# Hash attention and a gated feed-forward block: one pool of two-bank PSUM tiles for both phases, with sums and hashes sharing a tile

## The chip, the cores and the metric

The kernel runs on one core of one Trainium2 chip. The metric is the device time of one launch in microseconds (us). Five engines work side by side: TensorE (PE in the profile; its weight loads are PEld), VectorE (DVE), ScalarE (ACT), GpSimd (POOL) and SyncE (SP, which here only issues transfers). PSUM is the memory into which TensorE writes its results; it has eight banks of 512 fp32 values in each of 128 partitions. An instruction waits on semaphores for the instructions of other engines on which it depends.

## The reference

```python
# attention: B, H, S, D = 4, 8, 768, 64; proj is (64, 6)
q_bits = (np.einsum('bhsd,dk->bhsk', q, proj) > 0)          # the same for k
q_bucket = np.sum(q_bits * 2 ** np.arange(6), axis=-1)
mask = q_bucket[:, :, :, None] == k_bucket[:, :, None, :]
scores = np.where(mask, (1 / np.sqrt(D)) * np.matmul(q, k.transpose(0, 1, 3, 2)), -1e9)
attn = np.exp(scores - np.max(scores, axis=-1, keepdims=True))
attn = attn / (np.sum(attn, axis=-1, keepdims=True) + 1e-9)
x = np.matmul(attn, v).transpose(0, 2, 1, 3).reshape(3072, 512)
# feed-forward block: w_gate and w_val (512, 1536), w_out (1536, 512)
g = x @ w_gate
out = (g * (1 / (1 + np.exp(-g))) * (x @ w_val)) @ w_out
```

## The kernel before

The kernel has two phases, traced one after the other. The order in which each engine gets its instructions is the order of the program text (a manual schedule); every wait between engines is put in from the tiles that an instruction reads and writes. A pool hands out its tiles in turn from a fixed number of slots, and the first write into a slot waits for all users of the tile that had it before.

**Attention** goes over 16 pairs of heads (n = 0 to 15). A pair has 12 units: two halves of 384 query columns, and in each six chunks of 128 keys. Its PSUM pool has eight one-bank tiles (`bank`). An iteration n of the loop issues, in this order:

- for each of the 12 units `score`: `products` takes two bank tiles, one for each head, and writes q times k into them in fp32; `mark` adds a bf16 product of the hash bits, which shifts the pairs of unlike buckets out of reach, and then issues the exponential, one ACTIVATE of 384 columns for each head (L524), into a ring of 12 weight tiles A. Between the units, `add` sums these weights on VectorE;
- `total(n-1)`: matmuls with a column of ones reduce the sums of the pair before (`sum`, L578), ScalarE copies them to SBUF (`row`, L581), and transfers and a reciprocal on VectorE (`invert`) prepare the division (`norm`) for the next iteration;
- `prepare_pair(1)`, while there is a next pair: the hash matmuls of pair n+1 (`hps`, L423) into one bank tile, the signs on ScalarE (L428), a spread of the q bits by a transfer on POOL's queue (L440) and of the k bits on VectorE (L437);
- a step of the preparation of the feed-forward weights (`begin_pieces`, `advance_pieces`), which are split into three parts and kept in DRAM;
- for each of the 12 units `attend`: the weights times v (`av`, L539). Each half of a pair has a bank tile of its own, and ScalarE copies it to `xT` (L549) when its six chunks are done; `mean` (L548) is a small copy beside it.

The first pair is treated apart (`start_first`): it has transposes on TensorE (`tps`), and nine idle matmuls run ahead of them.

**The gated block** goes over three blocks of 1024 tokens. Each block has 12 steps U: the gate and the value product, each with a tile `a` (16 matmuls, the main parts) and a tile `n` (8 matmuls, the parts to be subtracted), then the evacuation, Silu and product, which leave `hid` in three parts h, l and d (L737, L740, L742). After each three steps there is a product D with `w_out`: eight chunks of 128 tokens, where `first` (six matmuls with h and l, into bank 0 of a tile `o`) and `second` (three with d, into bank 1) are evacuated by L785 and L789 on VectorE. In the last D of a block the first four chunks are begun ahead of time with two of the three `hid` tiles (`ahead` = 4), while the third is still being made. In the last D of all, chunks from the fifth on run `second` ahead of `first`, and the eighth (`last`) is worked in two halves of 256 columns, each with its own store (L816). This phase's PSUM pool has four two-bank tiles (`two_banks`), opened when the first phase's pool is closed.

Of the kernel before, what the change touches and what calls it, by code (L numbers as in the profile page):

```python
# [8 lines left out]
FP32 = mybir.dt.float32  # L9
# [10 lines left out]
def kernel(  # L20
# [54 lines left out]
    RINGS = (3, 3)  # L75
    ringp = [ctx.enter_context(tc.tile_pool(name="ringp", bufs=RINGS[0]))]
    dram = ctx.enter_context(tc.tile_pool(name="dram", bufs=1, space=bass.MemoryType.DRAM))
    ctx.enter_context(tc.manual_schedule())

    halves = [slice(half * HQ, (half + 1) * HQ) for half in range(2)]  # L80

# [216 lines left out]
    def attention(scope):  # L298
# [2 lines left out]
        fixed = scope.enter_context(tc.tile_pool(name="fixed", bufs=1))  # L301
        att = scope.enter_context(tc.tile_pool(name="att", bufs=2))
        xp = scope.enter_context(tc.tile_pool(name="xp", bufs=4))
        banks = scope.enter_context(tc.tile_pool(name="ps", bufs=8, space=PSUM))

        def bank(name):
            return banks.tile([P, 512], FP32, tag="ps", name=name)

        pairs = [(b, pr) for b in range(B) for pr in range(NP)]
        raws = {}  # L310
# [52 lines left out]
        nc.vector.memset(zeros, 0.0)  # L363
        for t in (sides["k", 0], sides["q", 0], sides["q", 1]):
            nc.vector.memset(t, 0.0)
        for _ in range(9):
            ps = bank("idle")
            nc.tensor.matmul(ps, zeros[:, 0:P], zeros[:, 0:512], start=True, stop=True)

        HR = 16  # L370
        assert 2 * NBITS <= HR and 2 * HR == BLOCK
# [40 lines left out]
        T = {}  # L412
        bits = {}

        def front(n):
            bits["q", n] = sides["q", n % 2]
            bits["k", n] = sides["k", n % 2]
            low, high = slice(0, BLOCK), slice(D, D + BLOCK)

            def hash_blocks(todo):  # L420
                tile_ = bank("hps")
                for i, (name, half) in enumerate(todo):
                    nc.tensor.matmul(tile_[i * BLOCK : (i + 1) * BLOCK, 0:HQ], hash_w,  # L423
                                     T[name, n][:, half * HQ : (half + 1) * HQ],
                                     start=True, stop=True)

                def sign(i, name, half, to=low, **how):
                    nc.scalar.activation(bits[name, n][to, half * HQ : (half + 1) * HQ],  # L428
                                         tile_[i * BLOCK : (i + 1) * BLOCK, 0:HQ], AF.Sign,
                                         **(how or {"bias": nudge[name]}))  # L430

                return [lambda i=i, at=at, **how: sign(i, *at, **how) for i, at in enumerate(todo)]
# [20 lines left out]
            def start_first():  # L453
                for half in range(2):
                    cols = slice(half * HQ, (half + 1) * HQ)
                    for name in "kq":
                        if not half:
                            T[name, n] = opnd.tile([P, S], FP32, tag=name + "T", name=name + "T")
                        ps = bank("tps")
                        for i in range(CH):  # L460
                            nc.tensor.transpose(ps[:, i * P : (i + 1) * P],
                                                raws[name, n][:, half * CH + i].rearrange("p h d -> p (h d)"),
                                                ident)
                        if name == "k":
                            nc.scalar.activation(T[name, n][:, cols], ps[:, 0:HQ], AF.Copy,
                                                 scale=2 / OFF)
                        else:
                            nc.vector.tensor_copy(T[name, n][:, cols], ps[:, 0:HQ])

                def both_heads(sign, name, half):  # L470
                    cols = slice(half * HQ, (half + 1) * HQ)
                    sign()
                    if name == "k":
                        spread_k(mask, cols)
                    else:
                        nc.vector.tensor_copy(bits["q", n][high, cols], bits["q", n][low, cols])

                products(0)
                todo = [("k", 0), ("q", 0), ("k", 1), ("q", 1)]
                signs = hash_blocks(todo)  # L480
                for i in range(3):
                    both_heads(signs[i], *todo[i])
                products(1)
                products(2)
                mark(0)
                both_heads(signs[3], *todo[3])
                mark(1)
                mark(2)

# [13 lines left out]
        def weights(u):  # L503
            return ring[u % RING]
# [3 lines left out]
        def product(u, x, start):  # L508
            n, half, c = units[u]
            qs = slice(half * HQ, (half + 1) * HQ)  # L510
            ks = slice(c * P, (c + 1) * P)
            for h in range(2):
                rows = slice(h * D, (h + 1) * D)
                nc.tensor.matmul(banks_of[u][h], x["k", n][rows, ks], x["q", n][rows, qs],  # L514
                                 start=start, stop=not start)

        def products(u):
            banks_of[u] = [bank("sc")[:, 0:HQ] for _ in range(2)]
            product(u, T, True)

        def mark(u):
            product(u, bits, False)
            for h, sc in enumerate(banks_of.pop(u)):
                nc.scalar.activation(weights(u)[:, h, 0:HQ], sc, AF.Exp,  # L524
                                     scale=SCALE * (1.0 if units[u][0] else OFF / 2))

        def score(u):
            products(u)
# [2 lines left out]
        def attend(u):  # L531
            n, half, c = units[u]
            a = weights(u)
            if c == 0:
                av[n] = bank("av")
            ps = av[n]
            width = AW if half == 0 else HQ
            for h in range(2):
                nc.tensor.matmul(ps[h * D : (h + 1) * D, 0:width], raws["v", n][:, h, c, :],  # L539
                                 a[:, h, 0:width], start=c == 0, stop=c == NCH - 1)  # L540
            if c == NCH - 1:
                if half == 0:
                    if n == len(pairs) - 1:
                        xT[n] = lastp.tile([P, S], FP32, tag="last", name="lastx")
                    else:
                        xT[n] = xp.tile([P, S], FP32, tag="xT", name="xT")
                    mean[n] = small.tile([P, 1], FP32, tag="e", name="e")
                    nc.scalar.activation(mean[n], ps[:, HQ : HQ + 1], AF.Copy, scale=EPS)  # L548
                nc.scalar.copy(xT[n][:, half * HQ : (half + 1) * HQ], ps[:, 0:HQ])  # L549

        both = {}

# [17 lines left out]
        sums = [dram.tile([P, each], FP32, tag=f"sums{i}", name="sums") for i in range(2)]  # L570

        def total(n):
            ps = bank("sum")
            t = [acc.pop((n, half)) for half in range(2)]
            for h in range(2):
                for half in range(2):
# [93 lines left out]
    def gated_block(scope):  # L670
# [2 lines left out]
        hidp = scope.enter_context(tc.tile_pool(name="hidp", bufs=4))  # L673
        outp = scope.enter_context(tc.tile_pool(name="outp", bufs=1))
        homes.append(outp)
        pp = scope.enter_context(tc.tile_pool(name="pp", bufs=4, space=PSUM))

        def two_banks(name):
            return pp.tile([P, 2, 512], FP32, tag="pp", name=name)

        hids = {}
        accs = {}
        rows = [out[b * S : (b + 1) * S, :].rearrange("(p c) m -> p c m", c=NCH) for b in range(B)]
# [2 lines left out]
        def mm(ps, w, x, start, stop):  # L686
            nc.tensor.matmul(ps, w, x, start=start, stop=stop)  # L687
# [27 lines left out]
        def atoms_of(kind, n):  # L715
# [33 lines left out]
            else:  # L749
# [2 lines left out]
                hs = [hids[NQ * n + j] for j in range(NQ)]  # L752
                tiles = {}

                def start(c, js):
                    if c not in tiles:
                        tiles[c] = two_banks("o")
                    t = tiles[c]
# [8 lines left out]
                        for j in js:  # L767
                            mm(t[:, 1], hs[j][:, 2, cols], ws[j][:, 2], j == 0, j == NQ - 1)

                    for go in (second, first) if final and c >= ahead else (first, second):  # L770
                        go()

                def end(c):
                    t = tiles.pop(c)
# [23 lines left out]
                for c in range(ahead):  # L798
                    yield lambda c=c: start(c, range(NQ - 1))
                def last(c):  # L800
                    t, tn = two_banks("o"), two_banks("o")
                    cols = slice(c * P, (c + 1) * P)
                    for j in range(NQ):
                        mm(tn[:, 0], hs[j][:, 2, cols], ws[j][:, 2], j == 0, j == NQ - 1)
                    nc.vector.tensor_tensor(accs[c], accs[c], tn[:, 0], op=ALU.subtract)
                    batch, at = divmod(b * NCB + c, NCH)
                    for half in range(2):
                        here = slice(half * DM // 2, (half + 1) * DM // 2)
                        for j in range(NQ):
                            for v in range(2):  # L810
                                mm(t[:, half, 0 : DM // 2], hs[j][:, v, cols], ws[j][:, v, here],
                                   j == 0 and v == 0, j == NQ - 1 and v == 1)
                        nc.vector.scalar_tensor_tensor(out=accs[c][:, here], in0=t[:, half, 0 : DM // 2],  # L813
                                                       scalar=STEP + 1, in1=accs[c][:, here],
                                                       op0=ALU.mult, op1=ALU.add)
                        nc.sync.dma_start(rows[batch][:, at, here], accs[c][:, here])  # L816

                for c in range(NCB):
# [2 lines left out]
                        return  # L821

                    def chunk(c=c):
                        start(c, [NQ - 1] if c < ahead else range(NQ))
                        end(c)
                    yield chunk

# [95 lines left out]
```

## Time and profile before

| | |
|---|---|
| median of 3 runs | 913.97 us (913.93 to 914.4) |
| profiled execution | 914.08 us |
| its span in the profile | 912.0 us, at a granted TensorE clock of 0.999 |
| TensorE busy | 904.2 us (99%) |
| VectorE busy | 667.2 us (73%) |
| ScalarE busy | 453.8 us (50%) |
| GpSimd busy | 97.0 us (11%) |
| attention phase | to 317.34 us, where the first matmul of the gated block starts |

The span runs from the first to the last record of the core; the execution's time has 2.1 us beside it. A row of the profile page names the line, engine, operation and tiles, then the busy time, the mean length of one, and the idle time of the engine ahead of it with what ended that. A row of the timeline has the start, the duration and what ran. The end of a matmul is modelled, and neighbours overlap: a matmul with 512 columns shows as 389 ns and follows the one before at 227 ns.

### The profile page before, as it was taken

To read this page: it belongs to the slowest core of one execution; us is meant where nothing else is said; L and a number is where in the kernel's file an instruction comes from. 1 tells how busy PE (TensorE), PEld (TensorE's weight loads), DVE (VectorE), ACT (ScalarE), POOL (GpSimd) and SP (SyncE) were. 2 spreads that over 40 slices of the span, in tenths; PEclk is the share of its full clock that TensorE was granted. 3 is DMA by queue.
4 is the path that set the end of the run, shared out by engine and by line. 5 is a ranking of instruction groups with operands and counts; after the bars stand their busy time and mean duration, and the time that the engine had idled before them with its cause. 6 is when DMAs were issued, how large, how long until landed. Compare 5 with 4: busy or idle time off the path is not lost.

```text
span 912.0 us, 12995 instructions
## 1 busy us (share of the span) xinstructions
PE 904.2 (99%) x4795; PEld 638.8 (70%) x4795; DVE 667.2 (73%) x774; ACT 453.8 (50%) x812; POOL 97.0 (11%) x193
## 2 busy tenths in 40 slices
PE   9999999999999999999999999999999999999997
PEld 5444444444444488888888788888888888888886
DVE  5999999998989768679776756464658754574746
ACT  6889888788887655452414133322313233313230
POOL 1011101010111210001000000101010100010000
PEclk9999999999999999999999999999999999999999
DMA  8677797778886699686756563434444642525232
GB/s 185 127 199 204 212 210 174 173 209 233 216 192 208 209 374 334 224 283 208 279 198 235 206 232 104 181 132 173 138 148 152 239 157 99 185 73 210 99 138 93
DMA packets 145582, 174.28 MB, mean 191 GB/s; under 512 B 106496, under 2 KB 115200, under 8 KB 145520
## 3 DMA queue, kind: packets, MB, share of 16 engines
q0 software_dynamic: 22864, 116.36, 36.4%
q1 hardware_dynamic: 121056, 56.71, 24.8%
q8 instruction: 38, 0.62, 0.3%
q10 hardware_dynamic: 1600, 0.39, 0.2%
q14 instruction: 24, 0.20, 0.1%
HBM read 133.17 MB, written 39.42 MB: 189 GB/s over the span
## 4 chain that ended last, share of the span: by engine, by line
PE 97%; DVE 2%; DMA 0%; ACTq 0%; ACT 0%; issue 0%; DVEq 0%
PE a L687 29%; PE o L687 20%; PE sc L514 17%; PE n L687 14%; PE av L539 14%; PE sum L578 1%; PE hps L423 1%; DMA kraw<-in_k_dram 0%; DVE hid L742 0%; DVE hid L740 0%; DVE v L732 0%; DVE v L736 0%; DVE xparts L292 0%; ACTq L329 0%; ACT hid L737 0%
## 5 line engine op out<-in xcount | busy, mean ns | idle before, releaser
L687 PE MATMUL a<-xparts,ring 128*128 128x512 f32 x1152 | 273.0, 389 | 0.6 <-ACT row L581 0.6
L687 PEld LDWEIGHTS a<-xparts,ring 128*128 128x128 f32 x1152 | 216.2, 188 | 46.2 <-ACT row L581 1.3
L687 PE MATMUL o<-ring,hid 128*128 128x512 f32 (+1 forms) x870 | 199.0, 388 | 2.3 <-DVE o L813 1.2
L687 PEld LDWEIGHTS o<-ring,hid 128*128 128x128 f32 x870 | 162.5, 188 | 37.2 <-DVE hid L742 2.4
L524 ACT ACTIVATE A<-sc 128x384 f32<-128x384 f32 x384 | 155.9, 504 | 8.1 <-PE sc L514 7.3
L514 PE MATMUL sc<-qT,kT 64*128 64x384 f32 x768 | 157.5, 488 | 0.0
L687 PE MATMUL n<-xparts,ring 128*128 128x512 f32 x576 | 142.3, 389 | 0.0
L539 PE MATMUL av<-A,vraw 128*64 128x386 f32 (+1 forms) x768 | 127.7, 488 | 0.0
L687 PEld LDWEIGHTS n<-xparts,ring 128*128 128x128 f32 x576 | 108.1, 188 | 22.4
L732 DVE TENSOR_TENSOR v<-v,n 128x1024 f32<-128x1024 f32 x36 | 44.0, 1221 | 99.4 <-PE n L687 98.8
L244 POOL DMA_DIRECT2D ring<-ram x108 | 56.9, 529 | 501.2 <-PE n L687 329.2
L539 PEld LDWEIGHTS av<-A,vraw 128*64 128x64 f32 x768 | 53.7, 137 | 73.3 <-issue 61.4
L514 PEld LDWEIGHTS sc<-qT,kT 64*128 64x128 f32 x768 | 70.3, 187 | 47.8 <-issue 41.9
L726 ACT ACTIVATE g<-a 128x1024 f32<-128x1024 f32 x36 | 36.9, 1026 | 132.1 <-PE a L687 127.2
L737 ACT ACTIVATE hid<-v 128x1024 fp32r<-128x1024 f32 x36 | 38.2, 1062 | 114.8 <-DVE v L736 114.8
L734 ACT ACTIVATE g<-g 128x1024 f32<-128x1024 f32 x36 | 38.2, 1061 | 85.2 <-DVE g L732 85.2
L789 DVE TENSOR_TENSOR o<-o 128x512 f32<-128x512 f32 x92 | 63.0, 687 | 20.6 <-ACT o L783 18.2
L732 DVE TENSOR_TENSOR g<-g,n 128x1024 f32<-128x1024 f32 x36 | 43.8, 1216 | 33.3 <-PE n L687 33.3
L514 PE MATMUL sc<-qb,kb 64*128 64x384 bf16 x384 | 66.0, 323 | 0.0
L560 DVE SCALAR_TENSOR_TENSOR both<-A 128x1536 f32<-128x1536 f32 x32 | 55.8, 1744 | 7.4 <-ACT A L524 6.1
L564 DVE TENSOR_TENSOR both<-both,A 128x1536 f32<-128x1536 f32 x32 | 56.2, 1757 | 3.2
L740 DVE SCALAR_TENSOR_TENSOR hid<-hid,v 128x1024 fp32r<-128x1024 f32 x36 | 44.0, 1223 | 19.2 <-ACT hid L737 19.1
(79 smaller groups left out, 701.0 us busy)
## 6 DMA issues: line engine op xcount, KB each, us to landing
ring<-ram POOLq DMA_DIRECT2D x108, 768.0 KB, 4.8
ram<-stage POOLq DMA_DIRECT2D x23, 768.0 KB, 5.6
ram<-stage SPq DMA_DIRECT2D x13, 768.0 KB
qraw<-in_q_dram SPq DMA_DIRECT2D x64, 96.0 KB
vraw<-in_v_dram SPq DMA_DIRECT2D x16, 384.0 KB
out_dram<-o SPq DMA_DIRECT2D x23, 256.0 KB
kraw<-in_k_dram SPq DMA_DIRECT2D x60, 96.0 KB
r<-sums SPq DMA_DIRECT2D x30, 192.0 KB
```

The costliest lines, as they stand in the source:

```text
L244: nc.gpsimd.dma_start(t.bitcast(FP32), ram[at].bitcast(FP32))
L514: nc.tensor.matmul(banks_of[u][h], x["k", n][rows, ks], x["q", n][rows, qs], start=start, stop=not start)
L524: nc.scalar.activation(weights(u)[:, h, 0:HQ], sc, AF.Exp, scale=SCALE * (1.0 if units[u][0] else OFF / 2))
L539: nc.tensor.matmul(ps[h * D : (h + 1) * D, 0:width], raws["v", n][:, h, c, :], a[:, h, 0:width], start=c == 0, stop=c == NCH - 1)
L560: nc.vector.scalar_tensor_tensor(out=t, in0=first, scalar=S * EPS / P / 2, in1=now, op0=ALU.add, op1=ALU.add)
L564: nc.vector.tensor_tensor(t, t, now, op=ALU.add)
L687: nc.tensor.matmul(ps, w, x, start=start, stop=stop)
L732: nc.vector.tensor_tensor(two(z), two(z), n_, op=ALU.subtract)
L734: nc.scalar.activation(z, z, AF.Silu)
L737: nc.scalar.activation(h, val, AF.Copy, scale=TOWARD / STEP)
L740: nc.vector.scalar_tensor_tensor(out=l, in0=h.bitcast(FP32), scalar=-STEP, in1=val, op0=ALU.mult, op1=ALU.add)
L789: nc.vector.tensor_tensor(accs[c], accs[c], t[:, 1], op=ALU.subtract)
```

## The change

The four two-bank tiles become the only PSUM pool, opened once for both phases.

- A unit of scores takes one such tile, a bank for each head, and one ACTIVATE of 768 columns makes the exponential of both.
- Both halves of `av` lie in one tile. `mean` and the copy to `xT`, now one of 768 columns, are issued after the last chunk of the second half.
- `joint(n)` is a tile that is made on first use. `total(n)` writes the sums of pair n into its bank 0, and the hash matmuls of pair n+2 go into its bank 1. In iteration n these are the sums of pair n-1 and the hashes of pair n+1, so both use `joint(n-1)`. The order of the calls in the loop is as before.
- The nine idle matmuls alternate between the banks of one tile, and each `tps` uses one bank of a tile.
- In the last D of each block, `first` of chunks 0 and 1 is completed ahead of `second` of chunk 0.
- `last` takes three tiles: one for the parts to be subtracted and one for each half.

```diff
+    pp = ctx.enter_context(tc.tile_pool(name="pp", bufs=4, space=PSUM))
     ctx.enter_context(tc.manual_schedule())
+
+    def two_banks(name):
+        return pp.tile([P, 2, 512], FP32, tag="pp", name=name)
...
-        banks = scope.enter_context(tc.tile_pool(name="ps", bufs=8, space=PSUM))
-
-        def bank(name):
-            return banks.tile([P, 512], FP32, tag="ps", name=name)
...
-        for _ in range(9):
-            ps = bank("idle")
-            nc.tensor.matmul(ps, zeros[:, 0:P], zeros[:, 0:512], start=True, stop=True)
+        idle = two_banks("idle")
+        for i in range(9):
+            nc.tensor.matmul(idle[:, i % 2], zeros[:, 0:P], zeros[:, 0:512], start=True, stop=True)
...
+        joints = {}
+
+        def joint(n):
+
+            if n not in joints:
+                joints[n] = two_banks("joint")
+            return joints[n]
+
         def front(n):
...
             def hash_blocks(todo):
-                tile_ = bank("hps")
+                tile_ = joint(n - 2)[:, 1]
...
-                        ps = bank("tps")
+                        ps = two_banks("tps")[:, 0]
...
-                nc.tensor.matmul(banks_of[u][h], x["k", n][rows, ks], x["q", n][rows, qs],
+                nc.tensor.matmul(banks_of[u][:, h], x["k", n][rows, ks], x["q", n][rows, qs],
                                  start=start, stop=not start)
 
         def products(u):
-            banks_of[u] = [bank("sc")[:, 0:HQ] for _ in range(2)]
+            banks_of[u] = two_banks("sc")[:, :, 0:HQ]
             product(u, T, True)
 
         def mark(u):
             product(u, bits, False)
-            for h, sc in enumerate(banks_of.pop(u)):
-                nc.scalar.activation(weights(u)[:, h, 0:HQ], sc, AF.Exp,
-                                     scale=SCALE * (1.0 if units[u][0] else OFF / 2))
+            nc.scalar.activation(weights(u)[:, :, 0:HQ], banks_of.pop(u), AF.Exp,
+                                 scale=SCALE * (1.0 if units[u][0] else OFF / 2))
...
-            if c == 0:
-                av[n] = bank("av")
-            ps = av[n]
+            if (half, c) == (0, 0):
+                av[n] = two_banks("av")
+            ps = av[n][:, half]
...
-            if c == NCH - 1:
-                if half == 0:
...
-                    mean[n] = small.tile([P, 1], FP32, tag="e", name="e")
-                    nc.scalar.activation(mean[n], ps[:, HQ : HQ + 1], AF.Copy, scale=EPS)
-                nc.scalar.copy(xT[n][:, half * HQ : (half + 1) * HQ], ps[:, 0:HQ])
+            if (half, c) == (1, NCH - 1):
...
+                mean[n] = small.tile([P, 1], FP32, tag="e", name="e")
+                nc.scalar.activation(mean[n], av[n][:, 0, HQ : HQ + 1], AF.Copy, scale=EPS)
+                nc.scalar.copy(xT[n].rearrange("p (x q) -> p x q", x=2), av[n][:, :, 0:HQ])
...
         def total(n):
-            ps = bank("sum")
+            ps = joint(n)[:, 0]
...
-        pp = scope.enter_context(tc.tile_pool(name="pp", bufs=4, space=PSUM))
-
-        def two_banks(name):
-            return pp.tile([P, 2, 512], FP32, tag="pp", name=name)
...
-                def start(c, js):
+                def start(c, js, steps=None):
...
-                    for go in (second, first) if final and c >= ahead else (first, second):
-                        go()
+                    for go in steps or ("ba" if final and c >= ahead else "ab"):
+                        (first if go == "a" else second)()
...
                 def last(c):
-                    t, tn = two_banks("o"), two_banks("o")
+                    tn, *ts = (two_banks("o")[:, 0] for _ in range(3))
...
-                        mm(tn[:, 0], hs[j][:, 2, cols], ws[j][:, 2], j == 0, j == NQ - 1)
-                    nc.vector.tensor_tensor(accs[c], accs[c], tn[:, 0], op=ALU.subtract)
+                        mm(tn, hs[j][:, 2, cols], ws[j][:, 2], j == 0, j == NQ - 1)
+                    nc.vector.tensor_tensor(accs[c], accs[c], tn, op=ALU.subtract)
...
-                                mm(t[:, half, 0 : DM // 2], hs[j][:, v, cols], ws[j][:, v, here],
+                                mm(ts[half][:, 0 : DM // 2], hs[j][:, v, cols], ws[j][:, v, here],
                                    j == 0 and v == 0, j == NQ - 1 and v == 1)
-                        nc.vector.scalar_tensor_tensor(out=accs[c][:, here], in0=t[:, half, 0 : DM // 2],
+                        nc.vector.scalar_tensor_tensor(out=accs[c][:, here], in0=ts[half][:, 0 : DM // 2],
...
                     def chunk(c=c):
-                        start(c, [NQ - 1] if c < ahead else range(NQ))
+                        if c >= ahead:
+                            start(c, range(NQ))
+                        elif c == 0:
+                            start(0, [NQ - 1], "a")
+                            start(1, [NQ - 1], "a")
+                            start(0, [NQ - 1], "b")
+                        else:
+                            start(c, [NQ - 1], "b" if c == 1 else "ab")
                         end(c)
```

More of the change, by code (lines that the diff above doesn't have):

```diff
@@ L540, in attend @@
                                  a[:, h, 0:width], start=c == 0, stop=c == NCH - 1)
-            if c == NCH - 1:
-                if half == 0:
[L543 to L546, printed above, removed]
-                    mean[n] = small.tile([P, 1], FP32, tag="e", name="e")
-                    nc.scalar.activation(mean[n], ps[:, HQ : HQ + 1], AF.Copy, scale=EPS)
-                nc.scalar.copy(xT[n][:, half * HQ : (half + 1) * HQ], ps[:, 0:HQ])
+            if (half, c) == (1, NCH - 1):
+                pool, tag = (xp, "xT") if n < len(pairs) - 1 else (lastp, "last")
+                xT[n] = pool.tile([P, S], FP32, tag=tag, name=tag)
+                mean[n] = small.tile([P, 1], FP32, tag="e", name="e")
+                nc.scalar.activation(mean[n], av[n][:, 0, HQ : HQ + 1], AF.Copy, scale=EPS)
+                nc.scalar.copy(xT[n].rearrange("p (x q) -> p x q", x=2), av[n][:, :, 0:HQ])
         both = {}
```

## The prediction

> **What bounds the kernel now.** I read the busy times first, then the waits of TensorE, then the timeline of one pair in the attention phase, of the handover between the phases, and of the end. From the profile page:
>
> ```profile
> PE 904.2 (99%) x4795; PEld 638.8 (70%) x4795; DVE 667.2 (73%) x774; ACT 453.8 (50%) x812; POOL 97.0 (11%) x193
> ...
> L524 ACT ACTIVATE A<-sc 128x384 f32<-128x384 f32 x384 | 155.9, 504 | 8.1 <-PE sc L514 7.3
> ```
>
> PE (TensorE) is busy for 904.2 of 912.0 us. Whatever relieves ACT (ScalarE), which is half idle, brings nothing by itself; a change counts only where it opens or closes a gap of PE. The waits of PE (engine, line waited for: us in total, times, longest) are these, apart from 0.3 us at the first transpose:
>
> ```profile
> PE idle L368 <- DVE kb L363: 1.3, 1, 1.3
> PE o L687 <- DVE o L813: 1.2, 1, 1.2
> PE o L687 <- DVE hid L742: 1.1, 3, 0.4
> PE a L687 <- ACT row L581: 0.6, 1, 0.6
> ```
>
> So the most that can be won is small: the last chunk (L813), the last product of each of three blocks (L742), the handover (L581). In the attention phase PE has no wait at all. The timeline of pair 7 (start, duration) shows how its engines hand over:
>
> ```profile
> 153.06 0.33 PE L514 MATMUL sc<-qb,kb 64*128 64x384 bf16 x2
> ...
> 153.32 0.85 PE L578 MATMUL sum<-acc,ones 128*32 128x384 f32 x8
> ...
> 153.99 0.49 PE L423 MATMUL hps<-qT,hash 128*32 128x384 f32 x2
> ...
> 154.31 0.48 ACT L581 COPY row<-sum 128x384 f32<-128x384 f32 x1
> ...
> 154.75 0.54 PE L539 MATMUL av<-A,vraw 128*64 128x386 f32 x2
> ```
>
> The reader is to see that the hash matmuls (hps) start at 153.99, 0.32 us **before** the copy that reads the sums (row) starts. The two lie in different tiles. Pairs 1 to 14 all show this order, with the row copy 0.95 to 0.99 us after the first sum matmul.
>
> Two places show what happens when PE meets a read of the tile it writes. At the end of the kernel:
>
> ```profile
> 907.31 0.42 DVE L813 SCALAR_TENSOR_TENSOR o<-o 128x256 f32<-128x256 f32 x1
> ...
> 907.79 0.98 PE L687 MATMUL o<-ring,hid 128*128 128x256 f32 x6 [1.24 <-DVE o L813]
> 908.81 0.42 DVE L813 SCALAR_TENSOR_TENSOR o<-o 128x256 f32<-128x256 f32 x1 [1.07 <-PE o L687]
> ```
>
> The first L813 reads bank 0 of tile t; the six matmuls write bank 1 of the same tile, and yet they start 0.06 us after that read ends. Two banks of one PSUM tile are thus **one object** for the waits. The handover gives the price of waiting for the row copy:
>
> ```profile
> 315.84 0.85 PE L578 MATMUL sum<-acc,ones 128*32 128x384 f32 x8
> 315.99 0.48 ACT L549 COPY lastx<-av 128x384 f32<-128x384 f32 x1 [3.35 <-PE av L539]
> 316.81 0.48 ACT L581 COPY row<-sum 128x384 f32<-128x384 f32 x1 [0.34 <-PE sum L578]
> ```
>
> followed by the first matmul of the second phase at 317.34: 1.50 us after the sums began, 0.05 after the copy ended.
>
> **What the Trainium skill says.** "PSUM — Partial Sum Buffer", section "PSUM bank collisions raise a hardware error", says that two engines on different banks run clean: the chip itself does not ask for a wait between two banks. The trace shows that this program waits all the same (L813), so the wait comes with the tile, and the measurement decides. "ScalarE: Activation LUTs", section "What ACT_TABLE_LOAD costs", gives an ACTIVATE with immediates 186 ns + 0.833 ns per column, and an overlap of about 93 ns for two back to back. The trace agrees: 384 columns would be 506 ns, measured 504, and 155.9 us/384 = 406 busy, an overlap of 98.
>
> **The change part by part.**
>
> 1. *Sums and hashes in one tile.* joint(n) holds the sums of pair n in bank 0 and the hashes of pair n + 2 in bank 1. In iteration n, total(n-1) issues the sum matmuls and the row copy, then prepare_pair issues the hash matmuls into joint(n-1), the same tile. By the L813 case they now wait for the row copy. Start of the sums to start of the hashes is 0.67 us now (153.32 to 153.99). With the wait it is 1.50, as in the handover: the row copy can't start sooner than about 0.97 after the sums, since it waits for their results, and takes 0.48. A stall of 0.83 us. Behind the hashes on PE stand the 48 av matmuls, then the next pair's scores; PE has nothing else, so all of it is lost. It occurs where an iteration has both a total and a next pair, n = 1 to 14: 14 x 0.83 = **+11.6 us**. The signs on ACT, the spreading DMA on POOL's queue and the k spread wait 0.83 longer too, but are needed only 8 us later, at the next scores.
>
> 2. *One exponential per unit.* 384 of 504 ns become 192 of an estimated 186 + 768 x 0.833 = 826 (733 back to back, against 2 x 406 = 812). A unit takes PE 0.81 us (153.06 back to 145.79 is nine units: 7.27/9). ACT thus keeps up; off the path, **0**. An exponential now needs both heads, but these finish together. Unit u + 4 needs the tile of unit u, 3.2 us after its start; its exponential ends 0.81 + 0.15 + 0.83 = 1.8 after it. Without the overlap ACT would fall behind by 0.02 per unit, 0.22 in twelve, and the row copy with it: upper end of the stall 1.05 us.
>
> 3. *One copy of both halves of xT.* 2 x 476 ns become about 0.83, plus the mean (0.17), at the end of the av matmuls. In pair 7 the second copy starts at 162.80 and the next exponential at 163.76, held by PE; mean and wide copy end at about 163.70. **0**; cover 0.06 us, and beyond it the four tiles. The av tile is needed by the fourth unit of scores, 2.4 us on. norm reads xT an iteration later.
>
> 4. *Start.* All first tiles now share four slots. The fourth unit of scores waits for one whole wide exponential, the others follow at 0.81. Worked through from the exponentials at 11.09 (unit 0) and the last sign at 11.98, the first hash for pair 1 comes at about 19.1 instead of 19.36: **-0.2**, bounds -0.4 and +0.4, as it hangs on estimated exponentials.
>
> 5. *One pool for both phases.* The first a takes the slot of a score tile long read, not that of the last sums. It can start 0.67 to 0.77 after 315.84, so at 316.55 instead of 317.34: **-0.8**. Its ACT evacuation was waiting for a DMA (r<-sums, until 321.44) and keeps that time; four tiles cover it. The weights for the third a are issued at 317.66, and land 9 to 16 us later in this stretch; they are needed at 328.37, now 0.8 sooner. That cover may be gone, so the lower end is -0.3.
>
> 6. *First two chunks interleaved.* In blocks 0 to 2 b(0) waits for L742 with two matmuls of a(0) done. Lost: about 0.5 us each (0.36 idle and the tail of a matmul, which shows as 389 ns at a pace of 227). Two more matmuls fill 0.45 of it; b(0) starts when it did. What is late next is chunk 4, which needs chunk 0's tile: it starts ten matmuls after b(0) now (505.71), eight after (505.26) then, but the read ends at 504.71 + 0.69 = 505.40. So 505.46: **-0.25** a block, -0.5 for the two blocks before the last.
>
> 7. *Last chunk in three tiles.* The wait for L813 goes. What is late next is DVE: end(6) starts at 904.97 (its pace from 902.31 is 1.33 a chunk) instead of 905.20, with the interleaving counted; L805 at 906.30, the halves at 907.08 and 907.52, the last ends at 907.94 instead of 909.23. The two stores on SP's queue (0.33 each) fit in between, but three transfers are now closer together: **-1.2**, bounds -0.7 and -1.3.
>
> Sum: +11.6 - 0.2 - 0.8 - 0.5 - 1.2 = +8.9. The profiled execution took 914.08, so 923.0; the median of the runs shown is 0.1 lower: **922.9 us**.
>
> **Rivals.**
>
> *A, the halves are told apart* (other side, faster): if the hash matmuls don't wait for a read of the other bank, part 1 is nothing and 914.0 - 2.7 = 911.3. It decides at a stall of 0.19 us a pair (2.7/14). For it: sum and hash are written by different helpers, and SBUF tiles show it (L785 writes the second half of an accumulator pair at 898.34, while the store of the first half, ahead of it in the program, is only issued at 898.45). Against it: L813, the same form in PSUM. Chance 0.07; another 0.01 for a part of the stall that leaves it within 0.2%, about what a measurement of this kernel can tell from no change.
>
> *B, ACT becomes late*: the wide exponentials don't overlap, the row copy comes up to 0.22 later, 14 x 1.05 = 14.7, so 926. For it: only 0.02 us a unit lie between 0.83 and 0.81. Against: the measured overlap. Chance 0.13.
>
> *C, a wait in each unit of scores*: four tiles don't suffice and PE loses 0.05 in each of 192 units, 9.6 more: 932. Against it, the slack of 1.4 us in part 2. Chance 0.05.
>
> *Main case*: 0.74.
>
> **How the numbers follow.** Faster by over 0.2% is A, 0.07; within 0.01; slower 0.92. Against the median, the main case spans 14 x 0.80 with savings of 3.2 (922.0) to 14 x 0.9 with savings of 1.0 (925.6); B reaches to 927. The range 921.2 to 926.8 goes 0.8 below the main case, for an error of 0.05 in fourteen stalls, takes in most of B and leaves out A, C and the tip.
>
> **What would show it.** A new wait of PE in hps for ACT row, 14 times some 0.65 to 0.85 us as the profile counts idle; the period of a pair at 20.06 instead of 19.23 us; a single wide exponential near 826 ns; no wait for L581 at the handover and none for L813; the chunk after the first four waiting for L789. If hps starts before row, part 1 is wrong and A holds.

## The result, and the profile after

| | before | changed |
|---|---|---|
| median | 914.18 us (913.93 to 914.69, 4 runs) | 924.16 us (923.94 to 924.34, 4 runs) |
| ratio to before | | 1.0108, interval 1.0091 to 1.0126 |
| profiled execution | 914.08 us | 923.94 us |
| its span | 912.0 us | 921.8 us |
| first matmul of the gated block | 317.34 us | 328.97 us |

The changed kernel is slower by 10.0 us; the forecast was 8.9 more. Iteration n of the attention loop, which the prediction calls pair n, issues the sums of pair n-1 and the hashes of pair n+1; below, iterations are counted. The line numbers of the changed kernel are some units off those of before: the scores are L522, the exponential L531, the sums L582, the row copy L585, the hashes L431, the av matmuls L546 and those of the gated block L686. Sums and hashes both go by the tile's name, joint. The busy times and the group of the exponential on the profile page of the changed kernel:

```profile
PE 905.9 (98%) x4795; PEld 634.2 (69%) x4795; DVE 667.8 (72%) x774; ACT 447.8 (49%) x604; POOL 97.0 (11%) x193
...
L531 ACT ACTIVATE A<-sc 128x768 f32<-128x768 f32 x192 | 151.7, 815 | 5.9 <-PE sc L522 2.5
```

PE has as many instructions as before and nearly the same busy time; what is new is time in which it does nothing. Its waits in the changed kernel (us in total, times, longest):

```profile
PE joint L431 <- ACT row L585: 9.5, 14, 0.8
PE idle L368 <- DVE kb L363: 1.3, 1, 1.3
PE tps L469 <- DMA kraw<-in_k_dram: 0.9, 1, 0.9
PE sc L522 <- ACT A L531: 0.6, 1, 0.6
```

Three of the four waits of before are gone from this list: L813, L742 and the handover (L581). Two are new. The hash matmuls wait for the row copy, 14 times, and once, in the first pair, the scores wait for an exponential (point 4 below). The wait for the transfer of kraw was there before with 0.3 us; in the runs below it lies between nothing and 1.0, so it is not counted for or against the change. In the timeline of iteration 7 of the changed kernel:

```profile
158.24 0.33 PE L522 MATMUL sc<-qb,kb 64*128 64x384 bf16 x2
158.50 0.85 PE L582 MATMUL joint<-acc,ones 128*32 128x384 f32 x8
159.49 0.48 ACT L585 COPY row<-joint 128x384 f32<-128x384 f32 x1
160.02 0.52 PE L431 MATMUL joint<-qT,hash 128*32 128x384 f32 x2 [0.67 <-ACT row L585]
...
160.80 7.98 PE L546 MATMUL av<-A,vraw 128*64 128x386 f32 x48
```

The order of row copy and hashes has turned round. The copy ends at 159.97 and the hashes start at 160.02, 1.52 us after the sums instead of 0.67. The 0.67 us that the wait shows is less than the loss, because the tail of the last sum matmul covers the rest. The mean length of an iteration, from the sums of iteration 1 (37.92) to those of iteration 15 (319.50), is 281.58/14 = 20.11 us; before it was (307.15 - 37.94)/14 = 19.23. So an iteration loses 0.88 on average, and 14 of them 12.4 us.

Where the other time went can be read from how far a stage's end is shifted against before. The handover comes 11.63 us later, the end of the last L742 (now L741, at 907.53) 11.11, the end of the last half of the last chunk (918.92) 9.69, the end of the profiled execution 9.86.

### The profile page after: what moved, and what is told of

It reads as the page before. It is cut to its first block, busy times and chain, and to the rows that moved or that the text cites. A ratio compares the mean times of both kernels' runs of the same rounds, so it can differ in the third digit from the quotient of the medians.

```text
span 921.8 us, 12624 instructions
## 1 busy us (share of the span) xinstructions
PE 905.9 (98%) x4795; PEld 634.2 (69%) x4795; DVE 667.8 (72%) x774; ACT 447.8 (49%) x604; POOL 97.0 (11%) x193
## 4 chain that ended last, share of the span: by engine, by line
PE 92%; ACT 3%; DMA 3%; SPq 1%; DVE 0%; issue 0%; ACTq 0%; DVEq 0%
PE a L686 28%; PE o L686 21%; PE n L686 14%; PE sc L522 14%; PE av L546 12%; ACT A L531 2%; PE joint L431 1%; SPq L337 1%; ACT row L585 1%; DMA r<-sums 1%; DMA few<-row 1%; DMA qraw<-in_q_dram 1%; DMA kraw<-in_k_dram 0%; DMA sums<-few 0%; DVE kT L459 0%
## 5 line engine op out<-in xcount | busy, mean ns | idle before, releaser
L686 PE MATMUL a<-xparts,ring 128*128 128x512 f32 x1152 | 273.0, 389 | 0.0
L686 PEld LDWEIGHTS a<-xparts,ring 128*128 128x128 f32 x1152 | 216.1, 188 | 45.5 <-issue 0.6
L686 PE MATMUL o<-ring,hid 128*128 128x512 f32 (+1 forms) x870 | 199.1, 389 | 0.0
L686 PEld LDWEIGHTS o<-ring,hid 128*128 128x128 f32 x870 | 162.1, 188 | 35.2 <-DVE hid L741 1.0
L522 PE MATMUL sc<-qT,kT 64*128 64x384 f32 x768 | 156.8, 487 | 0.6 <-ACT A L531 0.6
L531 ACT ACTIVATE A<-sc 128x768 f32<-128x768 f32 x192 | 151.7, 815 | 5.9 <-PE sc L522 2.5
L686 PE MATMUL n<-xparts,ring 128*128 128x512 f32 x576 | 142.2, 389 | 0.0
L546 PE MATMUL av<-A,vraw 128*64 128x386 f32 (+1 forms) x768 | 127.7, 488 | 0.0
L686 PEld LDWEIGHTS n<-xparts,ring 128*128 128x128 f32 x576 | 108.1, 188 | 22.4
L546 PEld LDWEIGHTS av<-A,vraw 128*64 128x64 f32 x768 | 53.7, 136 | 73.3 <-issue 72.7
L522 PEld LDWEIGHTS sc<-qT,kT 64*128 64x128 f32 x768 | 67.4, 187 | 49.4 <-issue 47.0
L522 PE MATMUL sc<-qb,kb 64*128 64x384 bf16 x384 | 63.1, 323 | 0.0
L739 DVE SCALAR_TENSOR_TENSOR hid<-hid,v 128x1024 fp32r<-128x1024 f32 x36 | 44.0, 1223 | 19.2 <-ACT hid L736 19.1
```

Source lines behind the costliest of these rows:

```text
L522: nc.tensor.matmul(banks_of[u][:, h], x["k", n][rows, ks], x["q", n][rows, qs], start=start, stop=not start)
L531: nc.scalar.activation(weights(u)[:, :, 0:HQ], banks_of.pop(u), AF.Exp, scale=SCALE * (1.0 if units[u][0] else OFF / 2))
L739: nc.vector.scalar_tensor_tensor(out=l, in0=h.bitcast(FP32), scalar=-STEP, in1=val, op0=ALU.mult, op1=ALU.add)
```

## The experiments

The theory: the two banks of a joint tile are one object for the waits, so a read of the sums that is issued ahead of the hash matmuls makes them wait. Rivals: ScalarE has become late with its wide exponentials; or four two-bank tiles are too few. Each run was timed beside runs of the kernel before, in three rounds, whose fastest runs of the kernel before are 913.76 to 913.87 us.

**The hashes in a tile of their own**

```diff
-                tile_ = joint(n - 2)[:, 1]
+                tile_ = two_banks("hps")[:, 0]
```

> The changed kernel, with the hashes in a two-bank tile of their own instead of bank 1 of the sums' tile; all else as changed. Shared-tile theory: the hash matmuls no longer wait for the row copy, the 14 stalls of 0.88 us go (12.4 us), and what is left is the gain of the other parts: 911.7 us, 0.3% faster than before; hps starts 0.67 us after the sums again and the period of a pair is 19.23 us. Late-ACT theory (the wide exponentials make the row copy late and that holds PE): the hashes don't wait for the row copy any more, but av or the next scores would; at least half of the 10 us stays, 917 or more. Few-tiles theory (four two-bank tiles are too few for sums, hashes, av and scores): one more tile in the turn makes it worse, 926 or more.

Measured: 911.71 us, ratio 0.9964 (0.9951 to 0.9976). Its timeline of iteration 7:

```profile
153.34 0.85 PE L582 MATMUL joint<-acc,ones 128*32 128x384 f32 x8
154.01 0.49 PE L431 MATMUL hps<-qT,hash 128*32 128x384 f32 x2
...
154.33 0.48 ACT L585 COPY row<-joint 128x384 f32<-128x384 f32 x1
...
154.77 2.49 PE L546 MATMUL av<-A,vraw 128*64 128x386 f32 x14
```

The hashes follow the sums at 0.67 us and precede the row copy again, with the wide exponential and the four tiles kept. One line of the change cost 12.4 us, and the rest of it gains. This version is faster than the changed kernel and, by some 0.3%, than the kernel before.

**Sums and hashes in one tile, the row copy behind the hashes**

```diff
                 q0, q1, *ks = hash_blocks(todo)
+                finish(reads)
                 q0()
...
         def total(n):
...
-            row = att.tile([P, HQ], FP32, tag="row", name="row", bufs=1)
-            nc.scalar.copy(row, ps[:, 0:HQ])
...
+            def read():
+                row = att.tile([P, HQ], FP32, tag="row", name="row", bufs=1)
+                nc.scalar.copy(row, ps[:, 0:HQ])
...
+            reads.append(read)
...
```

> The changed kernel, with sums and hashes in one tile as changed, but the row copy (and what follows from it) issued after the hash matmuls instead of ahead of them. Shared-tile theory: what costs is a read between two writes of one tile, not the sharing; without one between them the hashes follow the sums at 0.67 us and the time is 911.7 us, as with a tile of their own; the row copy starts some 0.7 us later after the sums, which nobody on TensorE waits for. If the sharing itself cost (two accumulations open in one tile, or the tile being free later), it stays near 924.

Measured: 911.91 us, ratio 0.9966 (0.9952 to 0.9979), the same as with a tile of their own. The timeline of iteration 7:

```profile
153.15 0.85 PE L584 MATMUL joint<-acc,ones 128*32 128x384 f32 x8
153.81 0.49 PE L431 MATMUL joint<-qT,hash 128*32 128x384 f32 x2
...
154.75 0.48 ACT L588 COPY row<-joint 128x384 f32<-128x384 f32 x1 [0.62 <-PE joint L431]
```

Sharing a tile costs nothing here as long as no read stands between the two writes. The other direction of the same rule shows as well: the row copy, which reads bank 0 alone, now waits for the hash matmuls in bank 1, and starts 1.60 us after the sums instead of 0.99. Nobody on PE waits for it. In all these traces the wait is one for a semaphore, so it is the program that asks for it; whether the chip would need it was not tested.

**The row copy twice**

```diff
-            nc.scalar.copy(row, ps[:, 0:HQ])
+            for _ in range(2):
+                nc.scalar.copy(row, ps[:, 0:HQ])
```

> The changed kernel, with the row copy issued twice, one after the other (the same data to the same place). Shared-tile theory: the hashes wait for the second copy, which ends about 0.4 us after the first (0.48 less the overlap of two ACTIVATEs): 14 x 0.4 = 5.6 us more, 929.8 us; PE's wait for ACT row grows from 0.67 to about 1.07 us each. Any theory in which the row copy is not what PE waits for: ScalarE is half idle, so within 1 us of 924.2.

Measured: 931.32 us, ratio 1.0178 (1.0164 to 1.0192), so 7.2 us more than the changed kernel. From the timeline of iteration 7:

```profile
162.02 0.85 PE L582 MATMUL joint<-acc,ones 128*32 128x384 f32 x8
163.01 0.99 ACT L586 COPY row<-joint 128x384 f32<-128x384 f32 x2
164.05 0.11 PEld L431 LDWEIGHTS joint<-qT,hash 128*32 128x32 f32 x2 [1.87 <-ACT row L586]
```

The hashes wait for the end of the second copy, as the theory has it; the size was off. The two copies take 0.99 us together and don't overlap, so each stall grew by 0.51 and not by 0.4: 14 x 0.51 = 7.1.

**The row copy twice, with the hashes in a tile of their own** (both diffs above)

> The changed kernel with the hashes in a tile of their own and the row copy issued twice. Shared-tile theory: nobody on TensorE waits for the row copy, so the same time as with one copy, within 0.5 us (911.7). If ScalarE's load in itself held TensorE up at this place, 2 us or more on top.

Measured: 911.69 us, against 911.71 with one copy. The same extra work on ScalarE costs 7.2 us where PE waits for it and nothing where it doesn't.

**Two narrow exponentials in the changed kernel**

```diff
-            nc.scalar.activation(weights(u)[:, :, 0:HQ], banks_of.pop(u), AF.Exp,
-                                 scale=SCALE * (1.0 if units[u][0] else OFF / 2))
+            t = banks_of.pop(u)
+            for h in range(2):
+                nc.scalar.activation(weights(u)[:, h, 0:HQ], t[:, h], AF.Exp,
+                                     scale=SCALE * (1.0 if units[u][0] else OFF / 2))
```

> The changed kernel, with the exponential of a unit again as two ACTIVATEs of 384 columns, one for each bank of the tile. Shared-tile theory: the stall at the hashes hangs on the row copy, which hangs on the sums' results and not on ScalarE's load: 924 us, within 0.8. Late-ACT theory: the wide exponential is what makes the row copy late, so the stalls shrink and the time falls by 3 us or more.

Measured: 924.31 us, ratio 1.0108 (1.0093 to 1.0124), against 924.16. The first row of PE's waits in this kernel:

```profile
PE joint L431 <- ACT row L587: 9.6, 14, 0.9
```

The stall is the same with either form, so the late-ACT theory falls as the cause of the stall.

**The shared tile alone, in the kernel before**

```diff
-        banks = scope.enter_context(tc.tile_pool(name="ps", bufs=8, space=PSUM))
+        banks = scope.enter_context(tc.tile_pool(name="ps", bufs=6, space=PSUM))
+        jp = scope.enter_context(tc.tile_pool(name="jp", bufs=1, space=PSUM))
...
-                tile_ = bank("hps")
+                tile_ = joint(n - 2)[:, 1]
...
-            ps = bank("sum")
+            ps = joint(n)[:, 0]
```

> The kernel before with one part of the change alone: sums and hashes in the two banks of one tile, which has two of the eight banks to itself; the other six stay a turn of one-bank tiles. Shared-tile theory: 14 stalls of 0.88 us on top of the time before, 926.6 us, with narrow exponentials and nothing else changed. Few-tiles theory (the stall needs the four two-bank tiles of the changed kernel): 914 to 915.

Measured: 926.86 us, ratio 1.014 (1.0123 to 1.0157). The control has the same six banks in the turn, and sums and hashes have tiles of their own:

```diff
...
-                tile_ = bank("hps")
+                tile_ = jp.tile([P, 512], FP32, tag="hps", name="hps")
...
-            ps = bank("sum")
+            ps = jp.tile([P, 512], FP32, tag="sum", name="sum")
```

> The kernel before with the same division of the banks (six in the turn, one for the sums, one for the hashes), but sums and hashes in two tiles. The control for the run beside it. Shared-tile theory: as before, 914.2 us, within 0.6. If six banks in the turn cost time in themselves, both runs are longer by the same amount.

Measured: 915.31 us, ratio 1.0013 (1.0006 to 1.002). This expectation failed: it is 1.3 us above the kernel before. From the first hashes of pair 0 to the first hashes of pair 1 it takes 11.84 us in both of these runs, and 11.03 in the kernel before. Six banks hold three units of scores and not four, and in the first pair, where the exponentials start late, PE's weight loads wait for them twice in the control, 0.48 and 0.59 us. That is 0.8 us at the start, and both runs have it. The profiled execution of the control lost another 0.5 once, between the sums of iterations 5 and 6 (19.76 us), where PE waited 0.4 for the k bits; why they were late stays open. With the shared tile the mean length of an iteration is (159.17 - 38.58)/6 = 20.10 us. So 926.86 is the time before (914.03 beside these runs), 14 stalls of 0.87, and the 0.7 that is left, for the start. The PE row of its waits:

```profile
PE joint L430 <- ACT row L588: 9.3, 14, 0.7
```

The stall comes without the wide exponential and without the four two-bank tiles. The few-tiles theory falls too, as far as the stall goes.

**The three gains, each undone on the version with the hashes apart (911.71 us)**

The last chunk in two tiles:

```diff
-                    tn, *ts = (two_banks("o")[:, 0] for _ in range(3))
+                    t, tn = two_banks("o"), two_banks("o")[:, 0]
+                    ts = [t[:, half] for half in range(2)]
```

> The hashes in a tile of their own, and the last chunk in two tiles as before (both halves in one). By the prediction's part 7 the wait of the last six matmuls for the first L812 comes back: 1.2 us more than 911.7, so 912.9. If the transfers at the end had hidden the wait, 911.7.

Measured: 912.68 us (912.52 to 913.3, 18 runs).

The first two chunks not interleaved:

```diff
-                        if c >= ahead:
...
-                            start(c, [NQ - 1], "b" if c == 1 else "ab")
+                        start(c, [NQ - 1] if c < ahead else range(NQ))
```

> The hashes in a tile of their own, and the first two chunks of a block's last product not interleaved (as before). By part 6: 0.25 us more for each of the first two blocks and 0.2 for the last, 0.7 in all: 912.4. If the wait of chunk 4 for chunk 0's tile takes all of the gain away, 911.7; if none, 913.1.

Measured: 912.47 us (912.28 to 912.93, 13 runs).

Two pools, one for each phase:

```diff
-    pp = ctx.enter_context(tc.tile_pool(name="pp", bufs=4, space=PSUM))
...
+        pps.append(scope.enter_context(tc.tile_pool(name="pa", bufs=4, space=PSUM)))
...
+        pps.append(scope.enter_context(tc.tile_pool(name="pp", bufs=4, space=PSUM)))
```

> The hashes in a tile of their own, and two pools of four two-bank tiles, one for each phase, in place of one. By part 5 the first matmul of the second phase waits for the last row copy again: 0.7 to 0.8 us more than 911.7, so 912.5. If the weights or the evacuation held the second phase back anyway, 911.7.

Measured: 912.47 us (912.31 to 913.24, 16 runs). The waits that came back, each from the waits of PE in its own kernel, in this order:

```profile
PE o L686 <- DVE o L813: 1.2, 1, 1.2
```

```profile
PE o L686 <- DVE hid L741: 1.1, 3, 0.4
```

```profile
PE a L689 <- ACT row L587: 0.6, 1, 0.6
```

These cost 0.97, 0.76 and 0.76 us. Each is the row of the kernel before, to 0.1 us, and each edit, undone alone, brings back its own wait and neither of the other two. The 911.71 us are from another round than these three runs, so a tenth of a microsecond in each is uncertain. Together they make 2.5 us, as much as lies between 911.71 and the 914.18 of before.

## Why the prediction was right, point by point

1. *Sums and hashes in one tile*: right in kind, place and number (14), a little short in size: 12.4 us against 11.6. Twelve of the stalls are 0.87, as the row copy starts 0.99 after the sums where 0.97 was taken, and what follows the hashes starts some 0.02 later than it used to. The first stall is 0.83. The one of iteration 14 is 1.03:

```profile
299.23 0.85 PE L582 MATMUL joint<-acc,ones 128*32 128x384 f32 x8
299.68 0.81 ACT L531 ACTIVATE A<-sc 128x768 f32<-128x768 f32 x1 [0.34 <-ACT A L531]
300.39 0.47 ACT L585 COPY row<-joint 128x384 f32<-128x384 f32 x1
...
300.91 0.52 PE L431 MATMUL joint<-qT,hash 128*32 128x384 f32 x2 [0.83 <-ACT row L585]
```

There the last exponential of the scores started 0.34 us after the one before it had ended, so the row copy was late, 1.16 after the sums. With the hashes in a tile of their own the copy is as late in the same iteration (1.15), and nobody waits for it. What held the exponential stays open; it is not its width, since the run with narrow ones has such a copy too (1.20). The stalls explain 0.7 us of the 1.1 by which the forecast was short (10.0 against 8.9); point 4 is the other 0.4.

2. *One exponential per unit*: no effect on the end, as forecast, shown by the run with narrow ones. A wide one takes 815 ns where 826 was estimated from the Trainium skill's "ScalarE: Activation LUTs", section "What ACT_TABLE_LOAD costs". ScalarE has 49% now; it was not what bound.

3. *One copy of xT*: from the first av matmul to the first score of the next pair it takes 7.91 us in both kernels, so nothing shows.

4. *Start*: this step failed in its sign. Forecast -0.2; from the transposes of the second half of k (6.46) to the first hashes of pair 1 (19.33) it is 12.87 us, before 12.66 (6.70 to 19.36), so **+0.2**. All runs with wide exponentials agree: from the first hashes of pair 0 to those of pair 1 they take 11.25 us, before 11.03. The wait itself was foreseen, that of the fourth unit for a whole exponential:

```profile
11.00 0.81 ACT L531 ACTIVATE A<-sc 128x768 f32<-128x768 f32 x1 [0.17 <-PE sc L522]
...
11.87 0.92 PE L522 MATMUL sc<-qT,kT 64*128 64x384 f32 x4 [0.58 <-ACT A L531]
```

Two terms were too short. That both heads "finish together" (part 2 of the prediction) does not hold at the start: the first wide exponential waits 0.17 us more for PE, which works on the bits of the second head after those of the first, and starts 2.92 us after the first hashes of pair 0 (8.08), where the first narrow one started after 2.76 (8.32 to 11.09). That is 0.16. And from the start of the fourth unit (11.87) to the hashes of pair 1 (19.33) it takes 7.46 us, while the prediction's own terms, an exponential from 11.09 with 0.83 us and hashes at 19.1, leave at most 7.2 for it. The working behind 19.1 is not given, so which of its units was short stays open. Before, the fourth unit had one bank free and began its first head at 11.23; only the second head (11.63) waited for an exponential. That head start of 0.9, counted from the first hashes of pair 0, was mostly used up by waits for the next ones, but not all. In the two profiled executions the transposes happened to start 0.24 apart, so the sums of iteration 1 come at nearly the same time (37.94 and 37.92), and the median hardly tells this point from nothing. "No wait at all" in the attention phase, as the prediction has it of before, is right for the loop; the 1.3 us of the idle matmuls and the 0.3 of the first transpose lie at its start.

5. *One pool*: right. The first a comes 0.78 us after the sums; the gain is 1.50 - 0.78 = 0.72 by the profile, and 0.76 by the run with two pools. In the changed kernel:

```profile
328.19 0.85 PE L582 MATMUL joint<-acc,ones 128*32 128x384 f32 x8
328.31 0.17 ACT L552 ACTIVATE e<-av 128x1 f32<-128x1 f32 x1 [5.15 <-PE av L546]
328.37 0.80 ACT L553 COPY last<-av 128x768 f32<-128x768 f32 x1
328.97 3.94 PE L686 MATMUL a<-xparts,ring 128*128 128x512 f32 x16
```

The a matmuls start in the middle of the copies, and no wait for weights followed, so the doubt about their cover did not come true.

6. *First two chunks interleaved*: right, and what is late next was right as well. In the changed kernel chunk 4's weights wait for the read of chunk 0's tile, 0.05 us past its end:

```profile
516.33 0.69 DVE L788 TENSOR_TENSOR o<-o 128x512 f32<-128x512 f32 x1
...
517.07 8.04 PEld L686 LDWEIGHTS o<-ring,hid 128*128 128x128 f32 x36 [0.31 <-DVE o L788]
```

Two blocks gained 11.63 - 11.11 = 0.52 us; forecast 0.5. The size is luck in part. Before, chunk 4 started at 505.88 and not at 505.71, as the pace gave, so its start gains more than 0.25; but after its new wait its second matmul comes 0.34 us after the first, where the pace is 0.23, and that takes part of it back.

7. *Last chunk in three tiles*: right. From the end of the last L742 to the end of the last read of PSUM it is 11.39 us instead of 12.81, a gain of 1.42 with the last block's interleaving (forecast 1.29, before the stores). From there to the end of the profiled execution it takes 0.17 longer than before (9.86 - 9.69), perhaps because the two stores now lie closer together; that was not tested:

```profile
918.16 0.76 DVE L812 SCALAR_TENSOR_TENSOR o<-o 128x256 f32<-128x256 f32 x2
918.62 0.81 SPq L815 DMA_DIRECT2D out_dram<-o  x2
```

With 11.11 - 9.86 = 1.25 in the profile, the forecast of 1.2 holds; undoing it alone cost 0.97.

The rivals: A would have been a kernel at 911.3 us. Its price was right, since 911.71 is what the change gives without the stall; but it needed the halves to be told apart, and the profile of before had shown at L813 that they aren't. B shows in one iteration of 14, by 0.16 us, and not for the reason given: the wide exponentials overlap and keep up. C leaves no trace: no unit of scores after the first pair waits.

## What to carry to other kernels

When two results are put into one PSUM tile, ask what the program reads between their writes: in this program a read of one bank holds the writes to the other, and a write to one holds the reads of the other. Put the reads behind the last write, or give the second result its own tile; both brought the 12.4 us back here. And a wait that the kernel already has, even one of 1.2 us at its very end, tells that a new edit of the same form will wait; the price was read from another place, the handover.

## What was not expected

Two copies on ScalarE of the same 384 columns to the same place took 0.99 us together, no overlap at all, where exponentials of 384 columns to different places take 0.504 each and 0.406 of busy time. The cause is not shown. The second copy writes what the first wrote, but the signs (L436), which write to different places, follow each other without overlap as well: 0.57 us each, 1.16 for two. And a turn of six PSUM banks in place of eight was not free in the kernel before: 1.3 us, 0.8 of it at the start.
